# When ten attention tiles are begun inside the blocks of a feed-forward layer: five and five for six and four

## The chip, the cores and the metric

The kernel runs on one core of a Trainium2 chip, in one launch. The metric is the device time of the launch in microseconds (us). The kernel before was run three times: 846.51, 847.0 and 848.07 us, median 847.0 us. One more execution, the profiled one, took 846.59 us, and all rows below are from it.

## The reference

Chunked attention on 4 x 8 heads of 576 tokens (chunks of 64), then two feed-forward layers on the 2304 tokens that it gives, the first with softplus, the second with a rational function:

```python
scores = scale * np.matmul(q_c, k_c.transpose(0, 1, 2, 4, 3))      # per chunk of 64 tokens
attn = softmax(scores)                                             # max taken off, sum + 1e-9
x = matmul(attn, v_c)          # -> (2304 tokens, 512)
h = x @ w_in                   # 512 -> 2048
g = np.maximum(h, 0.0) + np.log1p(np.exp(-np.abs(h)))              # layer 1
x = g @ w_out                  # 2048 -> 512
h = x @ w_in2; g = P(h) / (Q(h) + 1e-6); out = g @ w_out2          # layer 2
```

Everything is fp32 in and out.

## The kernel before

**Numbers.** Each fp32 operand of a matmul is held as a sum of two fp32r parts, hi and lo, and each product takes three terms (hi hi, hi lo, lo hi). `split` (L397) makes the parts: ACT copies hi (L407), DVE or POOL subtracts it from the source for lo (L415).

**Tiles and blocks.** Attention works on 18 tiles of 128 tokens (tile 0 to 17). Layer 1 works on blocks of 512, 512, 512, 384 and 384 tokens, that is on tiles 0-3, 4-7, 8-11, 12-14 and 15-17. Blocks one to three run one after the other, each in 16 steps (fc 0 to 15); the products of step s = 16 * block + fc are called h_s (h_0 to h_47): 12 matmuls into one of two PSUM banks. ACT then makes softplus of them twice (L1142 into t2, L1147 into g, the hi part), DVE or POOL subtracts for the lo part (L1150), and 12 matmuls add g_s into the accumulators (L1656, "acc"). Blocks four and five are done together after them as a pair, by a scheme that needs sums and differences of their x (operands T, xT_4) and of the weights (s24, S1, S3), made beforehand by DVE and ACT (L1166 to L1430), and multiplied on PE by L1463 (p and u). Layer 2 follows, with its own blocks.

**Attention.** Tiles 0 to 7 are done at the start and in block one. The others are begun inside the blocks: `attention(tb)` is called in the loop over blocks and steps at the steps that BEGIN_AT lists, as many in each block as BEGUN says. A tile's work runs through DVE, PE and ACT: q and k are turned, PE makes scores (L718, L731), DVE takes the maximum and subtracts it (L756, L766), ACT takes exp (L776), sums and a divide follow (L800 to L811), PE transposes the weights e (L818), ACT copies them out (L840, "aT"), PE multiplies them with v (L847, L859, "values") into the PSUM tile "aps", and `split` writes the values as a part of xT. `attention` leaves this second half as `unfinished`; it is added by `finish_attention`, which the next tile's `attention` calls. So the finish of tile n is added where tile n+1 begins.

**The buffers of xT.** A block's xT is one of two buffers of the pool `xpool` (L341). A new one is taken by the copy of the block's first tile (`new_x`). Block four's xT (named xT_3, its first part is tile 12) takes the buffer of block two's (xT_1), which the products h_16 to h_31 read.

**What sets the order.** No engine's order is written out. The class `Program` records each task with its engine, an assumed cost, the keys that it reads and writes and the buffers that it takes, in the order in which the code adds them. A key that is written makes the task depend on the key's writer and on the readers known so far; readers and writers added later are tied to the new writer. A list scheduler with a random search over priorities then sets the order on all engines at once (L83 to L299). So a change of where a tile is begun changes the dependencies that the planner sees, and can change the order from the first instruction on.

Of the kernel before, what the change touches and what calls it, by code (L numbers as in the profile page):

```python
# [43 lines left out]
LAST_FINISH = 12  # L44
LEAD = 0.0
LEAD2 = 0.0
BEGUN = (0, 6, 4)
BEGIN_AT = ((), (0, 3, 6, 9, 11, 14), (0, 3, 6, 9))
CONVERT = ((), (1, 2, 4, 5, 7, 8, 10, 11, 12, 14, 15), (1, 2, 3, 4, 5))
BACK = (0, 0, 1, *(1,) * 13)  # L50
QK_BY_VECTOR = {*range(18)} - {*STAGED}
# [251 lines left out]
def tile_chunk_attention_two_ffn(  # L303
# [1537 lines left out]
    def tiles_of(j):  # L1841
        t0, n = BLOCKS[j]
        return range(t0 // TB, (t0 + n) // TB)
# [12 lines left out]
    for bi, j in enumerate(ORDER1):  # L1856
        later = [t for n in (*ORDER1[bi + 1 :], *PAIR) for t in tiles_of(n) if t not in STAGED + begun]
        coming = later[: BEGUN[bi]]
        begun += tuple(coming)
        for fc in range(FC):  # L1860
            s += 1
            if coming and fc in BEGIN_AT[bi]:
                tb = coming.pop(0)
# [174 lines left out]
```

## Time and profile before

| | us |
|---|---|
| median of three runs | 847.0 |
| profiled execution, its own time | 846.59 |
| its span (first to last instruction) | 844.8 |
| PE busy | 828.2 |
| DVE busy | 609.8 |
| ACT busy | 525.9 |
| POOL busy | 221.8 |

The profiled execution's own time has 1.8 us around its span. PE is the engine of the matrix products; the other three make its operands. The waits of PE that are listed one by one, and the chain of waits followed back from the last instruction, tell where PE did not go on; a stretch of time is read in the timelines of the engines beside it.

### The profile page before, as it was taken

How to read it: one execution, taken by the hardware profiler on the slowest of the kernel's cores; microseconds unless marked ns; L12 is line 12 of the kernel's file. 1: busy time of each engine (PE TensorE's matmuls, PEld its weight loads, DVE VectorE, ACT ScalarE, POOL GpSimd, SP SyncE). 2: the span in 40 equal slices, each digit the busy share in tenths (PEclk: the TensorE clock that was granted, in tenths of full speed). 3: DMA queues.
4: the chain of work that ended last, by engine and by line, in shares of the span. 5: the costliest groups of instructions: out<-in, count | busy, mean ns of one | idle time of the engine just before them, and what ended most of it. 6: DMA issues, size and time to landing. Idle time of an engine off the chain costs nothing.

```text
span 844.8 us, 13339 instructions
## 1 busy us (share of the span) xinstructions
PE 828.2 (98%) x4984; PEld 707.1 (84%) x4984; DVE 609.8 (72%) x1070; ACT 525.9 (62%) x934; POOL 221.8 (26%) x205
## 2 busy tenths in 40 slices
PE   7999999999799999999999999999999999999998
PEld 6778888888588889999998888888889888888886
DVE  5778774775565867565288996877888886778784
ACT  5898983332232345556448797776678775667674
POOL 0000002232222332111011488332235161312131
PEclk9899999999999999999999999999999999999999
DMA  9985535565455201000383242200031000001001
GB/s 228 248 222 178 191 80 159 138 141 142 113 133 125 82 1 51 1 1 1 133 257 110 75 125 76 76 1 1 0 107 44 1 26 1 1 0 51 1 0 50
DMA packets 112401, 71.13 MB, mean 84 GB/s; under 512 B 81872, under 2 KB 99792, under 8 KB 112336
## 3 DMA queue, kind: packets, MB, share of 16 engines
q1 hardware_dynamic: 112336, 70.28, 30.4%
q8 instruction: 39, 0.64, 0.3%
q14 instruction: 26, 0.21, 0.1%
HBM read 56.63 MB, written 13.63 MB: 83 GB/s over the span
## 4 chain that ended last, share of the span: by engine, by line
PE 90%; ACT 5%; DVE 3%; DMA 1%; issue 1%; POOL 0%; ACTq 0%; POOLq 0%; DVEq 0%
PE h L1075 36%; PE acc L1689 22%; PE acc L1656 22%; PE u L1463 3%; PE p L1463 3%; ACT L370 1%; PE aps L847 1%; DMA wr_1o<-in_moe_w_out_dram 1%; DVE t L1563 1%; PE aps L679 1%; PE aps L718 1%; PE aps L859 1%; PE warm L1992 1%; PE aps L818 0%; ACT t L1142 0%
## 5 line engine op out<-in xcount | busy, mean ns | idle before, releaser
L1075 PE MATMUL h<-xT,w_2i 128*128 128x512 f32 (+1 forms) x960 | 209.1, 368 | 0.0
L1689 PE MATMUL acc<-w_2o,g 128*128 128x512 f32 x864 | 207.9, 390 | 0.1
L1075 PEld LDWEIGHTS h<-xT,w_2i 128*128 128x128 f32 x960 | 169.0, 188 | 31.3 <-ACT u L1560 0.2
L1689 PEld LDWEIGHTS acc<-w_2o,g 128*128 128x128 f32 x864 | 161.3, 188 | 33.3 <-DVE w_2o L415 0.5
L1656 PE MATMUL acc<-g,w_1o 128*128 128x512 f32 (+1 forms) x768 | 176.6, 378 | 0.0
L1593 POOL TENSOR_TENSOR g<-t,g 128x512 fp32r<-128x512 f32 (+1 forms) x80 | 95.2, 1190 | 243.7 <-ACT g L1590 194.9
L1656 PEld LDWEIGHTS acc<-g,w_1o 128*128 128x128 f32 x768 | 140.5, 188 | 22.3
L1075 PE MATMUL h<-xT,w_1i 128*128 128x512 f32 x564 | 137.0, 394 | 5.3 <-ACT g L1147 5.3
L1075 PEld LDWEIGHTS h<-xT,w_1i 128*128 128x128 f32 x564 | 106.2, 190 | 28.1 <-ACT g L1147 5.8
L1582 ACT ACTIVATE u<-t,row 128x512 f32<-128x512 f32 (+1 forms) x80 | 51.8, 649 | 34.7 <-DVE t L1563 33.7
L1607 ACT ACTIVATE t<-h,row 128x512 f32<-128x512 f32 (+1 forms) x80 | 58.5, 731 | 21.7 <-PE h L1075 21.3
L1563 DVE SCALAR_TENSOR_TENSOR t<-t,row,u 128x512 f32<-128x512 f32 (+1 forms) x80 | 55.2, 691 | 20.6 <-ACT u L1586 20.2
L1618 DVE TENSOR_TENSOR t<-h,t 128x512 f32<-128x512 f32 (+1 forms) x80 | 50.8, 635 | 26.4 <-ACT u L1560 9.6
L1150 POOL TENSOR_TENSOR g<-t,g 128x512 fp32r<-128x512 f32 x32 | 41.6, 1300 | 103.0 <-ACT g L1147 103.0
L1563 DVE SCALAR_TENSOR_TENSOR t<-u,row,t 128x512 f32<-128x512 f32 (+1 forms) x80 | 55.4, 693 | 14.0 <-ACT t L1578 6.9
L1563 DVE SCALAR_TENSOR_TENSOR t<-t,row,h 128x512 f32<-128x512 f32 (+1 forms) x80 | 55.4, 692 | 12.6 <-ACT t L1578 7.5
L1142 ACT ACTIVATE t<-h 128x512 f32<-128x512 f32 x48 | 28.7, 598 | 52.1 <-PE h L1075 51.8
L1578 ACT ACTIVATE t<-h,row 128x512 f32<-128x512 f32 (+1 forms) x80 | 51.2, 641 | 15.3 <-PE h L1075 8.9
L1590 ACT ACTIVATE g<-t 128x512 fp32r<-128x512 f32 (+1 forms) x80 | 46.5, 581 | 16.9 <-DVE t L1563 13.9
L1563 DVE SCALAR_TENSOR_TENSOR u<-t,row,u 128x512 f32<-128x512 f32 (+1 forms) x80 | 55.6, 696 | 0.0
L1147 ACT ACTIVATE g<-h 128x512 fp32r<-128x512 f32 x48 | 28.6, 598 | 42.9 <-PE acc L1656 42.9
L1560 ACT ACTIVATE u<-h 128x512 f32<-128x512 f32 (+1 forms) x80 | 43.4, 544 | 17.7 <-DVE t L1563 6.6
(156 smaller groups left out, 1024.3 us busy)
## 6 DMA issues: line engine op xcount, KB each, us to landing
wr_1i<-in_moe_w_in_dram SPq DMA_DIRECT2D x16, 512.0 KB, 4.7
wr_1o<-in_moe_w_out_dram SPq DMA_DIRECT2D x16, 512.0 KB, 5.0
wr_2i<-in_moe_w_in_dram SPq DMA_DIRECT2D x16, 512.0 KB, 4.7
wr_2o<-in_moe_w_out_dram SPq DMA_DIRECT2D x16, 512.0 KB, 4.8
out_dram<-ev SPq DMA_DIRECT2D x16, 256.0 KB, 2.3
x<-ev SPq DMA_DIRECT2D x6, 512.0 KB, 3.4
x2r<-x SPq DMA_DIRECT2D x6, 512.0 KB, 4.0
qk<-in_q_dram SPq DMA_DIRECT2D x80, 32.0 KB, 3.2
```

The lines of the kernel that those rows point to most:

```text
L1075: pe.matmul(hs[s], w[:, a, c * P : (c + 1) * P], xt[:, b, c, :n_tok], start=n == 0, stop=n == 3 * KC - 1,)
L1463: pe.matmul(banks[n], lhs(a, i, c), right(b, j, c), start=start and m == 0, stop=m == 5, skip_group_check=not start,)
L1560: act.activation(u(), h(), AF.Square)
L1563: return lambda: vec.scalar_tensor_tensor(out=out(), in0=in0(), scalar=scalar, in1=in1(), op0=op0, op1=op1)
L1578: act.activation(new("t1"), h(), AF.Abs, scale=b_t[:, 0:1])
L1582: act.activation(u(), d(), AF.Ln, bias=epsq_t)
L1590: act.activation(gs[s][:, 0, :n_tok], p(), AF.Copy)
L1593: pool.tensor_tensor(out=gs[s][:, 1, :n_tok], in0=p(), in1=gs[s][:, 0, :n_tok].bitcast(F32), op=ALU.subtract,)
L1607: lambda: act.activation(new("t2"), h(), AF.Identity, scale=na_t[:, 3:4], bias=na_t[:, 2:3]),
L1618: lambda: vec.tensor_tensor(out=p(), in0=h(), in1=p(), op=ALU.mult), [hkey, kp], [kp],
L1656: pe.matmul(accs[1, j, half][c % 2][:, :n_tok], wts[1, "o", fc][:, a, c * P : (c + 1) * P], gs[s][:, b, :n_tok], start=first and n == 0, s ...
L1689: pe.matmul(accs[2, j, half][c % 2], gs[s][:, b, c * P : (c + 1) * P], wts[2, "o", fc][:, a, :], start=first and n == 0, stop=last and n == 2,
```

## The change

Tiles 8 to 17 are the ten that are begun inside blocks two and three. Before, six began in block two, at steps 0, 3, 6, 9, 11 and 14, and four in block three, at steps 0, 3, 6 and 9. Now five begin in each: tiles 8 to 12 at steps 0, 3, 6, 9 and 12 of block two, tiles 13 to 17 at steps 0, 2, 4, 6 and 8 of block three. Tile 12 is begun a step later, tile 13 two steps later and in the next block; tile 14 is begun at step 2 instead of 0, tile 15 at 4 instead of 3, tile 16 stays at 6, and tile 17 begins at 8 instead of 9.

```diff
-BEGUN = (0, 6, 4)
-BEGIN_AT = ((), (0, 3, 6, 9, 11, 14), (0, 3, 6, 9))
+BEGUN = (0, 5, 5)
+BEGIN_AT = ((), (0, 3, 6, 9, 12), (0, 2, 4, 6, 8))
```

No instruction of the computation is added or removed; the table loads of ACT (L370) are 23 instead of 25, and the small matmuls that keep PE going at the start (L1992) stand in another place. The planner's order differs on every engine. Three places follow.

**Around tile 12's copy, ACT.** The copy of tile 12's values into block four's xT (L407, xT_3), before: t2 and g are the softplus outputs of the products of the same number, cm_2i and cm_2o conversions of layer 2's weights, e_13 the exp of tile 13.

```order
L470 ACTIVATE cm_2o_12_2399<-wr_2o_12_2335 128x512
L407 ACTIVATE xT_3_2408<-aps_513 128x4x128
L776 ACTIVATE e_13_2442<-e_13_2442,row_97 128x512
L1142 ACTIVATE t2_30_2464<-h_1_30_2428 128x512
L1147 ACTIVATE g_30_2468<-h_1_30_2428 128x512
L1147 ACTIVATE g_31_2490<-h_1_31_2449 128x512
L1142 ACTIVATE t2_31_2492<-h_1_31_2449 128x512
```

And now:

```order
L1142 ACTIVATE t2_30_2368<-h_1_30_2332 128x512
L1142 ACTIVATE t2_31_2385<-h_1_31_2354 128x512
L470 ACTIVATE cm_2i_13_2401<-wr_2i_13_2371 128x512
L1147 ACTIVATE g_30_2413<-h_1_30_2332 128x512
L1147 ACTIVATE g_31_2446<-h_1_31_2354 128x512
L1142 ACTIVATE t2_32_2462<-h_1_32_2433 128x512
L1147 ACTIVATE g_32_2488<-h_1_32_2433 128x512
L470 ACTIVATE cm_2o_13_2491<-wr_2o_13_2464 128x512
L1142 ACTIVATE t2_33_2501<-h_1_33_2475 128x512
L1728 ACTIVATE ev_1_1_0_2510<-acc_1_1_0_1580 128x512
L1728 ACTIVATE ev_1_1_1_2547<-acc_1_1_1_0_1610 128x512
L1147 ACTIVATE g_33_2552<-h_1_33_2475 128x512
L407 ACTIVATE xT_3_2571<-aps_497 128x4x128
```

The copy xT_3 stood ahead of the softplus of h_30 and h_31; now it stands behind the last of g_33. The conversion cm_2o_12 stands in front of t2_30 in the one as in the other.

**The same place, PE.** Here aT_12 and v_12 give the values of tile 12, qkT_13 the scores of tile 13. Before:

```order
L847 MATMUL aps_513<-aT_12_2323,v_12_2294 64x64 x16
L718 MATMUL aps_513<-qkT_13_2291 64x64 x16
L1656 MATMUL acc_1_1_0_1620<-g_29_2346,w_1o_13_1352 128x512 x6
L1656 MATMUL acc_1_1_1_0_1604<-g_29_2346,w_1o_13_1352 128x512 x3
L1656 MATMUL acc_1_1_1_1_1605<-g_29_2346,w_1o_13_1352 128x512 x3
L1075 MATMUL h_1_30_2428<-xT_1_770,w_1i_14_1350 128x512 x12
L1075 MATMUL h_1_31_2449<-xT_1_770,w_1i_15_1417 128x512 x12
L1075 MATMUL h_1_32_2477<-xT_2_1745,w_1i_0_121 128x512 x12
L1656 MATMUL acc_1_1_1_0_1604<-g_30_2468,w_1o_14_1424 128x512 x3
```

And now:

```order
L1075 MATMUL h_1_30_2332<-xT_1_802,w_1i_14_1366 128x512 x12
L1075 MATMUL h_1_31_2354<-xT_1_802,w_1i_15_1439 128x512 x12
L1656 MATMUL acc_1_1_0_1580<-g_28_2265,w_1o_12_1324 128x512 x6
L1656 MATMUL acc_1_1_1_0_1610<-g_28_2265,w_1o_12_1324 128x512 x3
L1656 MATMUL acc_1_1_1_1_1611<-g_28_2265,w_1o_12_1324 128x512 x3
L1656 MATMUL acc_1_1_0_1580<-g_29_2346,w_1o_13_1373 128x512 x6
L1656 MATMUL acc_1_1_1_0_1610<-g_29_2346,w_1o_13_1373 128x512 x3
L1656 MATMUL acc_1_1_1_1_1611<-g_29_2346,w_1o_13_1373 128x512 x3
L1075 MATMUL h_1_32_2433<-xT_2_1796,w_1i_0_121 128x512 x12
```

The values of tile 12 stood ahead of h_30 and are no longer among these rows (they come after the sums of g_31); between h_31 and h_32 there was nothing, and now there are six groups of sums (24 matmuls).

**Block one, around the transposes of tile 6 (L679).** On PE the transposes of e_5 (L818) come first, then sums, then those of tile 6, which take the same PSUM tile. Before:

```order
L818 MATMUL aps_513<-ident_96,e_5_772 128x128 x4
L1656 MATMUL acc_1_0_1_0_589<-g_4_780,w_1o_4_784 128x512 x3
L1656 MATMUL acc_1_0_1_1_590<-g_4_780,w_1o_4_784 128x512 x3
L679 MATMUL aps_513<-ident_96,qk_6_119 128x128 x8
L1075 MATMUL h_1_6_865<-xT_0_331,w_1i_6_127 128x512 x12
```

And now:

```order
L818 MATMUL aps_497<-ident_96,e_5_797 128x128 x4
L1656 MATMUL acc_1_0_1_0_558<-g_4_799,w_1o_4_785 128x512 x3
L1656 MATMUL acc_1_0_1_1_559<-g_4_799,w_1o_4_785 128x512 x3
L1656 MATMUL acc_1_0_0_578<-g_4_799,w_1o_4_785 128x512 x6
L679 MATMUL aps_497<-ident_96,qk_6_119 128x128 x8
L1656 MATMUL acc_1_0_1_0_558<-g_5_852,w_1o_5_847 128x512 x3
```

Three groups of sums (12 matmuls) stand between the two transposes instead of two (6 matmuls). On ACT, from the exp of tile 5 to the copy aT_5 that empties that PSUM tile, before:

```order
L776 ACTIVATE e_5_772<-e_5_772,row_97 128x512
L370 ACT_TABLE_LOAD
L468 ACTIVATE cm_1i_6_802<-wr_1i_6_683 128x512
L468 ACTIVATE cm_1o_5_805<-wr_1o_5_713 128x512
L468 ACTIVATE cm_1i_7_813<-wr_1i_7_759 128x512
L468 ACTIVATE cm_1o_6_815<-wr_1o_6_782 128x512
L370 ACT_TABLE_LOAD
L1147 ACTIVATE g_5_827<-h_1_5_789 128x512
L407 ACTIVATE w_1i_6_127<-cm_1i_6_802 128x512
L840 ACTIVATE aT_5_846<-aps_513 128x512
```

And now:

```order
L776 ACTIVATE e_5_797<-e_5_797,row_97 128x512
L370 ACT_TABLE_LOAD
L468 ACTIVATE cm_1i_7_825<-wr_1i_7_773 128x512
L468 ACTIVATE cm_1o_6_828<-wr_1o_6_787 128x512
L407 ACTIVATE w_1o_5_847<-cm_1o_5_730 128x512
L370 ACT_TABLE_LOAD
L1147 ACTIVATE g_5_852<-h_1_5_806 128x512
L1142 ACTIVATE t2_5_861<-h_1_5_806 128x512
L840 ACTIVATE aT_5_870<-aps_497 128x512
```

Four weight conversions (L468) stood there and now two, and one hi copy of a weight (L407) and one softplus (L1142) stand on other sides of the copy than before.

**The end of block three, PE.** From the values of tile 17 (aT_17), the last tile, on (p and u are products of the pair). Before:

```order
L847 MATMUL aps_513<-aT_17_3305,v_17_3184 64x64 x16
L1075 MATMUL h_1_47_3356<-xT_2_1745,w_1i_15_1417 128x512 x12
L1656 MATMUL acc_1_2_1_0_2615<-g_44_3294,w_1o_12_1332 128x512 x3
L1656 MATMUL acc_1_2_1_1_2616<-g_44_3294,w_1o_12_1332 128x512 x3
L1656 MATMUL acc_1_2_0_2604<-g_45_3321,w_1o_13_1352 128x512 x6
L1656 MATMUL acc_1_2_1_0_2615<-g_45_3321,w_1o_13_1352 128x512 x3
L1656 MATMUL acc_1_2_1_1_2616<-g_45_3321,w_1o_13_1352 128x512 x3
L1463 MATMUL p_0_0_3417<-xT_3_2408,w_1i_0_121 128x384 x6
L1656 MATMUL acc_1_2_0_2604<-g_46_3400,w_1o_14_1424 128x512 x6
L1656 MATMUL acc_1_2_1_0_2615<-g_46_3400,w_1o_14_1424 128x512 x3
L1656 MATMUL acc_1_2_1_1_2616<-g_46_3400,w_1o_14_1424 128x512 x3
L1656 MATMUL acc_1_2_0_2604<-g_47_3424,w_1o_15_1476 128x512 x6
```

And now:

```order
L847 MATMUL aps_497<-aT_17_3337,v_17_3226 64x64 x16
L1656 MATMUL acc_1_2_1_0_2583<-g_45_3323,w_1o_13_1373 128x512 x3
L1656 MATMUL acc_1_2_1_1_2584<-g_45_3323,w_1o_13_1373 128x512 x3
L1656 MATMUL acc_1_2_0_2600<-g_46_3379,w_1o_14_1446 128x512 x6
L1656 MATMUL acc_1_2_1_0_2583<-g_46_3379,w_1o_14_1446 128x512 x3
L1656 MATMUL acc_1_2_1_1_2584<-g_46_3379,w_1o_14_1446 128x512 x3
L1656 MATMUL acc_1_2_0_2600<-g_47_3418,w_1o_15_1457 128x512 x6
L1656 MATMUL acc_1_2_1_0_2583<-g_47_3418,w_1o_15_1457 128x512 x3
L1656 MATMUL acc_1_2_1_1_2584<-g_47_3418,w_1o_15_1457 128x512 x3
L1463 MATMUL p_0_0_3456<-xT_3_2571,w_1i_0_121 128x384 x6
L1463 MATMUL u0_3473<-xT_3_2571,w_1i_2_123 128x384 x6
L1463 MATMUL p_0_1_3485<-xT_3_2571,w_1i_0_121 128x384 x6
```

The values of tile 17 stand behind h_47 instead of ahead of it and behind sums of g_45; after the rows shown, before, come six more sums of g_47, then u0, six products of T2, six of xT_3 and six of T3 ahead of the first product that reads xT_4, and now u1 alone stands ahead of that product.

At the start, two subtractions of DVE (L766) for the fourth starting tile stand behind the divide of the second (L811), where they stood ahead of it, and all 24 pieces of h_0 (L1100) stand behind the last starting tile's values (L859), where 8 stood ahead of them.

## Rows read from the trace of the kernel before

**Rows 1.** Head of the page: span; busy us, share and instructions of PE.
```profile
span 844.8 us, 13339 instructions
...
PE 828.2 (98%) x4984; PEld 707.1 (84%) x4984; DVE 609.8 (72%) x1070; ACT 525.9 (62%) x934; POOL 221.8 (26%) x205
```

**Rows 2.** Section 4 of the page: the chain of waits, shares by engine.
```profile
PE 90%; ACT 5%; DVE 3%; DMA 1%; issue 1%; POOL 0%; ACTq 0%; POOLq 0%; DVEq 0%
```

**Rows 3.** Waits of PE: who waits, releaser, us in total, times, longest.
```profile
PE h L1075 <- ACT g L1147: 5.3, 1, 5.3
PE aps L818 <- DVE room L811: 2.6, 1, 2.6
...
PE aps L679 <- ACT aT L840: 0.8, 1, 0.8
```

**Rows 4.** The chain in order of time: start us, us, what.
```profile
210.00 5.45 PE h L1075 x24
...
219.66 0.58 ACT t L1142
...
220.78 4.50 PE h L1075 x12
```

**Rows 5.** ACT's timeline: start us, us, instruction, [idle <- releaser].
```profile
207.28 0.68 ACT L470 ACTIVATE cm_2o<-wr_2o 128x512 f32<-128x512 f32 x1 [2.21 <-DMA w2i<-cm_2i]
215.48 0.60 ACT L407 ACTIVATE xT<-aps 128x512 fp32r<-128x512 f32 x1 [7.52 <-PE h L1075]
219.03 0.72 ACT L776 ACTIVATE e<-e,row 128x512 f32<-128x512 f32 x1 [2.95 <-DVE e L766]
```

**Rows 6.** Windows: PE, PEld, DVE, ACT, POOL busy us, PEclk, DMA share, GB/s.
```profile
221.00:223.00 2.00, 2.00 (x5) 1.61 (x6) 1.31 (x2) 1.36 (x3) 1.66 (x2) 0.50 0.78 127
...
225.00:229.00 4.00, 4.00 (x20) 3.28 (x19) 3.80 (x8) 1.20 (x2) 0.21 (x1) 1.00 0.73 172
```

**Rows 7.** PE's timeline, block one, around the transposes of tile 6.
```profile
60.26 1.64 PE L1656 MATMUL acc<-g,w_1o 128*128 128x512 f32 x6
62.74 1.09 PE L679 MATMUL aps<-ident,qk 128*128 128x128 f32 x8 [0.85 <-ACT aT L840]
```

**Rows 8.** ACT's timeline, the same stretch.
```profile
57.42 0.68 ACT L468 ACTIVATE cm_1i<-wr_1i 128x512 f32<-128x512 f32 x1
...
59.79 1.28 ACT L370 ACT_TABLE_LOAD   x1
...
62.10 0.59 ACT L840 ACTIVATE aT<-aps 128x512 f32<-128x512 f32 x1
```

**Rows 9.** DVE's timeline at the start.
```profile
16.88 0.41 DVE L766 TENSOR_TENSOR room<-aps,mx 128x256 f32<-128x256 f32 x1
```

**Rows 10.** ACT's timeline at the start.
```profile
24.36 0.60 ACT L840 ACTIVATE room<-aps 128x512 f32<-128x512 f32 x1 [0.42 <-PE aps L818]
```

**Rows 11.** PE's timeline at the start.
```profile
23.98 2.06 PE L1100 MATMUL h<-xT,w_1i 128*128 128x256 f32 x8
25.96 0.69 PE L859 MATMUL aps<-room,v 64*64 64x64 f32 x32
26.59 2.04 PE L1100 MATMUL h<-xT,w_1i 128*128 128x256 f32 x12
28.99 0.74 PE L1100 MATMUL h<-xT,w_1i 128*128 128x256 f32 x4 [0.36 <-DVE xT L1006]
```

**Rows 12.** PE's timeline before the pair of blocks.
```profile
308.03 0.69 PE L847 MATMUL aps<-aT,v 64*64 64x64 f32 x32
```

**Rows 13.** DVE's timeline before the pair of blocks.
```profile
313.38 2.39 DVE L1368 TENSOR_TENSOR r<-w_1i 128x512 f32<-128x512 f32 x2
...
318.07 0.68 DVE L1269 TENSOR_TENSOR xT<-xb,xT 128x512 fp32r<-128x512 f32 x1
...
322.87 0.69 DVE L1368 TENSOR_TENSOR r<-w_1i 128x512 f32<-128x512 f32 x1
```

**Rows 14.** POOL's timeline, the same stretch.
```profile
313.87 1.36 POOL L1150 TENSOR_TENSOR g<-t,g 128x512 fp32r<-128x512 f32 x1 [7.85 <-ACT g L1147]
```

## The prediction

> **What bounds the kernel now.** I read the head of the page first: PE is busy for 828.2 of a span of 844.8 us [rows 1]. The chain of waits agrees, 90% PE, 5% ACT, 3% DVE [rows 2]. With 16.6 us of the span not PE's, a change of order alone can only win in the places where PE stands still, or lose by making new ones. So the next view is the list of PE's waits. One of them is far larger than the rest after the start: 5.3 us ahead of a product h, with ACT's softplus g named as the releaser. Of the others, 2.6 us are the start's, for DVE's divide, and 0.8 us is a wait of the transposes L679 for ACT's copy aT [rows 3].
>
> The chain in order of time shows how the 5.3 us come about. PE works on h_30 and h_31 until 210.00 + 5.45 = 215.45. Then the chain leaves PE: the softplus of h_30 starts only at 219.66, and PE goes on at 220.78 with h_32, which needs one of the two banks of h_30 and h_31 [rows 4]. ACT had nothing to do meanwhile: its copy into xT stood at the head of its queue and waited 7.52 us for PE's h. Behind it stood tile 13's exp, which waited another 2.95 us for DVE's subtraction of the maximum, and only then the softplus of h_30 [rows 5]. So this is a ring. The copy takes the buffer that h_30 and h_31 read, and cannot start before h_31 ends; the softplus that would free the banks is queued behind the copy, although h_30 was ready 2.7 us earlier.
>
> The stop costs more than its idle time. The windows show a granted clock of 0.50 from 221 to 223, the lower of the two levels (1.2 of 2.4 GHz), after PE had idled, and 1.00 again from 225 [rows 6]. h_32 takes 4.50 us, while h_30 and h_31 take 5.45 together, 2.72 each [rows 4].
>
> **The change part by part.**
>
> *The ring.* Before, tile 13 was begun at step 14 of block two, so tile 12's finish, with the copy into xT_3, was recorded before h_30 and h_31 were. The planner then knew of no reading of the old buffer by these two, and put ACT's copy ahead of their softplus. The chip's semaphores hold it all the same. Now tile 13 begins at step 0 of block three, behind all sixteen products of block two, and the order shows the copy behind g_33's softplus. t2_30 and g_30 stand with nothing of tile 12 or 13 ahead of them. What goes is the idle time, 220.78 - 215.45 = 5.33 us, and the slow clock, 4.50 - 2.72 = 1.78 us: **-7.1 us**.
>
> What is late next there? h_32 needs the bank of h_30. In the new order h_31 (2.72 us) and 24 matmuls of sums (24 x 0.227 = 5.45 us, by 5.45 / 24 from [rows 4]) stand between the end of h_30 and h_32: 8.2 us of work. ACT needs for t2_30, t2_31, a conversion and g_30 four times about 0.6 us, 2.4 us. The cover is some 5.8 us, so I take the whole sum. The copy itself, later now, holds only the values of tile 12, which nobody needs before the pair of blocks. Bounds: -7.1 if the cover holds, 0 if something else holds ACT there for the same time.
>
> *Block one.* PE's six matmuls of sums from 60.26 would end at 61.62 (6 x 0.227), and the transposes start at 62.74 [rows 7]: 1.12 us lost. They wait for the PSUM tile that ACT's copy aT empties at 62.10 to 62.69. Ahead of the copy ACT does four conversions (the first at 57.42), a table load of 1.28 us, and softplus [rows 8]. Now two of the four conversions are gone from there, a second softplus has come in, and PE has 12 sums to do, 2.72 us instead of 1.36. PE gains 1.36 of cover and ACT about one instruction of 0.56 us, together 1.9 us against 1.12 lost: **-1.1 us**, with 0 as the other bound, if the later h_5 or DVE's part of tile 5 is what ends last.
>
> *The start.* In DVE's queue two subtractions of 0.41 us [rows 9] go behind the divide of the second starting tile, for which PE waited 2.6 us [rows 3]; it comes about 0.7 us earlier. In exchange eight pieces of h_0, which took 2.06 us [rows 11] while ACT's copy was still to come, go behind the last starting tile's values. That copy ended at 24.36 + 0.60 = 24.96 [rows 10], the pieces at 25.96, so the values can start 1.0 us earlier, and 24 pieces instead of 16 follow. At 2.04 / 12 = 0.17 us a piece [rows 11] h_0 would end at 24.96 + 0.63 + 24 x 0.17 = 29.67, which is where it ends now (28.99 + 4 x 0.17). Of the 0.7 us I believe half, since some conversions moved ahead of the last tile's divide: **-0.4 us**. Bounds: -1.1 us (all of the 0.7, and the 0.36 of waiting in [rows 11]) and +1.7 us (24 pieces at the 2.06 / 8 = 0.26 of the first eight cost 2.1 more, less the 0.4).
>
> *The end of block three.* From the values of tile 17 at 308.03 [rows 12] DVE and ACT make the operands of the pair, the last of them xT's lo part at 318.07 + 0.68 [rows 13]: 10.7 us. Before, PE had 54 matmuls of 0.227 us and 30 of 128x384 (0.227 x 384 / 512 = 0.17 us each) in that time, 17.4 us by the order, before the first product that reads xT_4. Now the values stand behind h_47: 30 sums (6.8 us) and 24 small products (4.1 us) remain, 10.9 us. The margin falls from 6.7 us to 0.2. Against that the operands S and s24 are asked for in another order. I take **+0.4 us**: at most a small wait, since the chain of 10.7 holds work for other operands that the new order can put behind. Bounds: 0 and about +3.
>
> Row and rule here: two subtractions of DVE took 2.39 us while POOL made a softplus's lo part beside them, from 313.87 on [rows 14]; one alone takes 0.69 [rows 13]. The Trainium skill, "GPSIMD Engine Reference", section "1. Specifications", says that GpSimd shares its SBUF interfaces with VectorE, with contention for DVE instructions that have two SBUF inputs, as these have; the trace agrees. It speaks against the change: tile 17's operands are subtractions of that sort, and they now run nearer to the softplus of h_46 and h_47.
>
> *All the rest* (blocks two and three besides, the pair, layer 2) is reordered without a visible cost: PE had hardly a wait there, and the new order has no two products of h that stand closer than others did before. I take 0, with +-1 us for small waits that come or go.
>
> Sum: 846.59 - 7.1 - 1.1 - 0.4 + 0.4 = 838.4 us for an execution like the profiled one. The median is 847.0, 0.4 more, so the forecast is **838.8 us**. All terms at their good ends give 846.6 - 7.1 - 1.1 - 1.1 - 1 + 0.4 = 836.7.
>
> **The rivals.**
>
> *The pair of blocks waits.* The margin of 0.2 us does not hold: DVE's chain behind tile 17's values is stretched by POOL's lo parts, by 1.1 us for each that falls on two subtractions (2.39 less twice about 0.65). With two or three of them PE waits 2 to 3 us ahead of the first product with xT_4; and as the stop at 215 shows, PE's clock may fall after it and cost up to 1.8 more. Time: 841 to 843.5 us, say 842. For it: the order has values later, and five tiles in block three. Against it: products that don't need xT_4 are at hand, and the searching planner puts them in front.
>
> *The change does not do what it says.* The copy is free, but ACT is held elsewhere by another instruction at the head of its queue, such as the exp of a tile that waits for DVE (2.95 us before, [rows 5]), and PE stands for as long as before: 845.3 to 848.7, about 847. Against it: the cover of 5.8 us.
>
> *Slower: the conversion in front of the softplus.* cm_2o_12 stands right ahead of t2_30 in the new order. It waits for a DMA, and ACT waits in order; one such wait was 2.2 us, just before the copy [rows 5]. PE waits for what its lateness exceeds the cover of 5.8 us by, and 1.8 us go to the clock. Slower than before by 1.7 us it is from 5.8 + 8.2 (the sum of the four terms) + 1.7 - 1.8 = 13.9 us on; at 15 us the time is 838.8 + 9.2 + 1.8 = 849.8, about 850. Against it: no wait of that kind was longer than 2.2 us.
>
> **How the numbers follow.** Three runs of before span 1.6 us, and 0.2% (1.7 us) is about what can be told from no change. The forecast has 0.72, with its own range 836.5 to 840.5; the pair's wait 0.15; no change 0.07; slower 0.06. The first two are faster by over 0.2%: 0.87. The range leaves out the last two and a little at the low end: 836 to 843.5 us.
>
> **What would show it.** In the list of PE's waits the row h <- g of 5.3 us is gone, the windows around the passage from block two to three have a clock of 1.00 throughout, and h_32 takes 2.7 us. ACT's copy of tile 12 starts without a long wait. The row L679 <- aT of 0.8 us is gone. At the end of block three a wait of p (L1463) for DVE's xT, s or S of up to 0.5 us agrees with my term; 2 us or more is the first rival. PE's busy time falls by about 1.8 us and the span by about 8. The forecast is wrong if a wait of over 3 us stands anywhere after the start, or if the copy of xT_3 is still ahead of a softplus for which PE waits.

## The result and the profile after

The changed kernel takes 840.08 us (median of four runs, 839.73 to 840.27), the kernel before 847.48 us in the same comparison (846.51 to 848.07): a ratio of 0.9913, 95% interval 0.9896 to 0.993. It is 7.4 us faster; the forecast was 838.8 us, 1.3 us too low, within its range. In a later comparison the same two took 841.22 and 847.24 us, a ratio of 0.993 (0.9918 to 0.9943).

The head of the page after, section 4 (the chain of waits by engine) and PE's waits (who waits, releaser, us in total, times, longest) answer to [rows 1 to 3]:

```profile
span 838.0 us, 13379 instructions
...
PE 827.4 (99%) x5004; PEld 707.6 (84%) x5004; DVE 611.0 (73%) x1070; ACT 523.2 (62%) x932; POOL 224.0 (27%) x205
```

```profile
PE 96%; SPq 1%; ACT 1%; DMA 1%; DVE 0%; issue 0%
```

```profile
PE aps L818 <- DVE room L811: 2.0, 1, 2.0
PE warm L1992 <- DVE xT L415: 1.4, 1, 1.4
...
PE aps L859 <- ACT room L840: 0.9, 2, 0.7
PE p L1463 <- ACT u L1484: 0.6, 1, 0.6
```

The chain is on PE for 96% instead of 90%, and ACT's share has gone from 5% to 1%. The wait of h for g (5.3 us) and that of L679 for aT (0.8 us) are gone. Two are new: the small matmuls "warm" wait 1.4 us for DVE at the start, and the pair of blocks 0.6 us. PE's instructions are 5004 instead of 4984, and all 20 are such small matmuls: the section on the change says that they stand in another place, but there are 48 of them instead of 28. The program counts them from the gaps that the planner leaves on PE before the first h.

PE's timeline at the passage to block three (start us, us, instruction) answers to [rows 4]:

```profile
203.39 5.60 PE L1075 MATMUL h<-xT,w_1i 128*128 128x512 f32 x24
208.83 5.60 PE L1656 MATMUL acc<-g,w_1o 128*128 128x512 f32 x24
214.27 2.88 PE L1075 MATMUL h<-xT,w_1i 128*128 128x512 f32 x12
216.99 2.88 PE L1656 MATMUL acc<-g,w_1o 128*128 128x512 f32 x12
```

h_30 and h_31 are followed by 24 matmuls of sums and by h_32 without a gap. On ACT, answering to [rows 5]:

```profile
204.33 0.66 ACT L470 ACTIVATE cm_2o<-wr_2o 128x512 f32<-128x512 f32 x1
206.31 0.60 ACT L1142 ACTIVATE t<-h 128x512 f32<-128x512 f32 x1 [1.32 <-PE h L1075]
...
226.47 0.60 ACT L407 ACTIVATE xT<-aps 128x512 fp32r<-128x512 f32 x1 [0.47 <-PE aps L718]
```

The softplus of h_30 starts when its products end, and the copy of tile 12 comes 23 us after the start of h_30 instead of 5.6, with a wait of 0.47 us instead of 7.52. The windows (PE, PEld, DVE, ACT, POOL busy us, PEclk, DMA share, GB/s) show the full clock there, where [rows 6] had 0.50:

```profile
209.00:215.00 6.00, 6.00 (x28) 4.95 (x28) 5.80 (x11) 2.21 (x4) 1.62 (x1) 1.00 0.40 73
215.00:221.00 6.00, 6.00 (x28) 4.99 (x27) 1.06 (x2) 1.75 (x4) 1.66 (x2) 1.00 0.52 155
```

**Where the time went.** The profiled executions have spans of 844.8 and 838.0 us, 6.8 apart. I compare them at points where PE has done the same work of the computation.

| stretch | before | after | difference |
|---|---|---|---|
| end of h_0 | 29.57 | 30.97 | +1.4 |
| start of tile 6's transposes (after: 65.87 less 2.72 for h_6, which stands ahead of them now) | 62.74 | 63.15 | +0.4, so block one -1.0 |
| start of h_30 to end of h_32 (after: less the 24 sums, 5.44) | 225.11 - 209.84 = 15.27 | 216.99 - 203.39 - 5.44 = 8.16 | -7.1 |
| all the rest | | | -0.1 |

Block one answers to [rows 7]: the transposes (L679) follow the sums without a wait.

```profile
62.66 0.60 PE L818 MATMUL aps<-ident,e 128*128 128x128 f32 x4
63.01 3.02 PE L1656 MATMUL acc<-g,w_1o 128*128 128x512 f32 x12
65.87 1.03 PE L679 MATMUL aps<-ident,qk 128*128 128x128 f32 x8
```

On ACT ([rows 8]) the copy that frees their PSUM tile ends at 63.89, two microseconds before they start:

```profile
60.94 1.28 ACT L370 ACT_TABLE_LOAD   x1
62.24 0.60 ACT L1147 ACTIVATE g<-h 128x512 fp32r<-128x512 f32 x1
62.73 0.59 ACT L1142 ACTIVATE t<-h 128x512 f32<-128x512 f32 x1
63.29 0.60 ACT L840 ACTIVATE aT<-aps 128x512 f32<-128x512 f32 x1
```

The start, PE's timeline, answers to [rows 11]:

```profile
17.30 0.65 PE L818 MATMUL aps<-ident,room 128*128 128x128 f32 x4 [1.96 <-DVE room L811]
...
21.21 2.07 PE L1992 MATMUL warm<-ident 128*128 128x128 f32 x8 [1.44 <-DVE xT L415]
23.08 1.06 PE L818 MATMUL aps<-ident,room 128*128 128x128 f32 x4
...
27.90 3.23 PE L1100 MATMUL h<-xT,w_1i 128*128 128x256 f32 x24
30.97 1.04 PE L679 MATMUL aps<-ident,qk 128*128 128x128 f32 x8
```

The second starting tile's transposes come at 17.30 instead of 17.95. But behind its values stand eight small matmuls, which write the PSUM tile of these values and so wait for DVE's subtraction that reads it; the third tile's transposes follow at 23.08, 5.78 us after the second's, where they came 2.41 us after them before (17.95 and 20.36).

### The profile page after: what moved, and what is told of

The parts are those of the page before. It is cut to its first block, busy times and chain, and to the rows that moved or that the text cites. A ratio compares the mean times of both kernels' runs of the same rounds, so it can differ in the third digit from the quotient of the medians.

```text
span 838.0 us, 13379 instructions
## 1 busy us (share of the span) xinstructions
PE 827.4 (99%) x5004; PEld 707.6 (84%) x5004; DVE 611.0 (73%) x1070; ACT 523.2 (62%) x932; POOL 224.0 (27%) x205
## 4 chain that ended last, share of the span: by engine, by line
PE 96%; SPq 1%; ACT 1%; DMA 1%; DVE 0%; issue 0%
PE h L1075 39%; PE acc L1656 24%; PE acc L1689 23%; PE p L1463 3%; PE u L1463 3%; SPq L622 1%; PE aps L847 1%; DMA wr_1i<-in_moe_w_in_dram 1%; PE aps L718 1%; PE aps L859 0%; PE aps L679 0%; PE warm L1992 0%; PE h L1100 0%; PE aps L818 0%; SPq L643 0%; PE aps L731 0%
## 5 line engine op out<-in xcount | busy, mean ns | idle before, releaser
L1075 PE MATMUL h<-xT,w_1i 128*128 128x512 f32 x564 | 135.2, 391 | 0.0
L1150 POOL TENSOR_TENSOR g<-t,g 128x512 fp32r<-128x512 f32 x32 | 43.6, 1362 | 126.1 <-ACT g L1147 126.1
L1142 ACT ACTIVATE t<-h 128x512 f32<-128x512 f32 x48 | 28.6, 596 | 59.4 <-PE h L1075 59.2
```

Source lines behind the costliest of these rows:

```text
L1075: pe.matmul(hs[s], w[:, a, c * P : (c + 1) * P], xt[:, b, c, :n_tok], start=n == 0, stop=n == 3 * KC - 1,)
L1150: (vec if by_vector else pool).tensor_tensor(out=gs[s][:, 1, :n_tok], in0=t["t2"], in1=gs[s][:, 0, :n_tok].bitcast(F32), op=ALU.subtract,)
```

## The experiments

My theory is the ring: tile 12's finish is recorded ahead of the products h_30 and h_31, so ACT's copy stands ahead of the softplus that PE needs, while it waits for PE. The rivals are that the even spread of the tiles pays, that tile 13's exp behind the copy was the real stop, and that the new search of the planner was lucky.

**e1: the ring put back into the changed kernel.**

```diff
-BEGUN = (0, 5, 5)
-BEGIN_AT = ((), (0, 3, 6, 9, 12), (0, 2, 4, 6, 8))
+BEGUN = (0, 6, 4)
+BEGIN_AT = ((), (0, 3, 6, 9, 12, 14), (2, 4, 6, 8))
```

> The changed kernel with tile 13 begun at step 14 of block two again (six and four tiles; all other places as in the changed kernel). Theory (the ring: tile 12's finish is recorded ahead of h_30 and h_31, so ACT's copy xT_3 stands ahead of their softplus): the wait of h for g of about 5.3 us at the passage to block three is back, with a slow h_32 behind it, and the time is 7.1 us above the changed kernel's 840.1, about 847 us. Rival (the gain comes from spreading the tiles five and five, or from the new search as a whole): no wait above 2 us there, 839 to 842 us.

It took 846.18 us, 0.9982 of before (0.9973 to 0.9991), a little under the expected 847. The stop is back, as PE's timeline and then ACT's show:

```profile
209.54 5.60 PE L1075 MATMUL h<-xT,w_1i 128*128 128x512 f32 x24
219.66 4.61 PE L1075 MATMUL h<-xT,w_1i 128*128 128x512 f32 x12 [4.52 <-ACT g L1147]
```

```profile
215.18 0.60 ACT L407 ACTIVATE xT<-aps 128x512 fp32r<-128x512 f32 x1 [6.19 <-PE h L1075]
...
218.54 0.58 ACT L1142 ACTIVATE t<-h 128x512 f32<-128x512 f32 x1
```

The copy again stands ahead of the softplus of h_30, and h_32 again takes 4.61 us. 4.52 + 4.61 - 2.72 = 6.4 us are lost, near the 6.1 by which its median stands above the changed kernel's.

**e2: before, with two instructions moved.** `done[12]` is DVE's subtraction of tile 12's values, the task ahead of it ACT's copy. Both have to go: in DVE's queue the subtraction stood ahead of tile 13's maximum, which tile 13's exp needs, and waited 8.37 us for the copy.

```diff
-        for i, t in prog.schedule():
+        order = prog.schedule()
+        late = [o for o in order if o[0] in (done[12] - 1, done[12])]
+        order = [o for o in order if o not in late]
+        at = [i for i, t in order].index(g31) + 1      # g31: ACT's task for g_31
+        order[at:at] = late
+        for i, t in order:
```

> The kernel before with its own order on every engine, but for two instructions: the copy of tile 12's values into xT_3 (ACT) and its subtraction (DVE) are issued behind g_31 instead of ahead of t2_30. Theory (ring): the wait of 5.3 us and the slow h_32 go, nothing else moves, 847.5 - 7.1 = 840.4 us; ACT's copy waits for less than 1 us. Rival (the stop has another cause, such as tile 13's exp that waits for DVE, which stays ahead of t2_30): PE still stands for 2 to 5 us, 843 to 847 us.

839.68 us, 0.9907 of before (0.9892 to 0.9922), where the ring said 840.4. This shows the cause: begin steps, search and the rest of the order are those of before, and the gain is there. PE's timeline and ACT's:

```profile
210.46 8.32 PE L1075 MATMUL h<-xT,w_1i 128*128 128x512 f32 x36
218.62 4.24 PE L1656 MATMUL acc<-g,w_1o 128*128 128x512 f32 x18
```

```profile
211.47 0.73 ACT L776 ACTIVATE e<-e,row 128x512 f32<-128x512 f32 x1 [1.15 <-DVE e L766]
...
213.88 0.59 ACT L1147 ACTIVATE g<-h 128x512 fp32r<-128x512 f32 x1
216.16 0.60 ACT L1147 ACTIVATE g<-h 128x512 fp32r<-128x512 f32 x1 [1.69 <-PE h L1075]
216.66 0.59 ACT L407 ACTIVATE xT<-aps 128x512 fp32r<-128x512 f32 x1
```

h_30, h_31 and h_32 are one run of 36 matmuls, 8.16 us from start to start of what follows, against 15.27 before: -7.1 us to the tenth. Tile 13's exp stands ahead of the softplus as before and does no harm, since it no longer comes behind the copy. One other wait moved: that of L679 for aT in block one was 1.67 us here, with the order of before, where it had been 0.85.

**e3: tile 13 alone moved** in the kernel before (tile 14 makes room by one step).

```diff
-BEGIN_AT = ((), (0, 3, 6, 9, 11, 14), (0, 3, 6, 9))
+BEGIN_AT = ((), (0, 3, 6, 9, 11), (0, 1, 3, 6, 9))
```

> The kernel before with tile 13 alone moved: begun at step 0 of block three, tile 14 at step 1 to make room; tiles 12 and 15 to 17 stay where they were. Theory (ring): 847.5 - 7.1 = 840.4, with 1.5 us to either side for what the search finds elsewhere: 839 to 842 us, no wait of PE above 1 us after the start. Rival (the regular spacing of the tiles in block three matters as well): ACT and DVE are late with tiles 13 and 14 begun one step apart, waits of 2 us or more in block three, 843 us or more.

839.43 us, 0.9912 (0.9898 to 0.9925), and no wait above 0.8 us behind the start. In these times the places of tiles 12 and 15 to 17 win nothing; the section on e4, e7 and e8 looks behind the start.

**e9: tile 13 one step later** in the kernel before.

```diff
-BEGIN_AT = ((), (0, 3, 6, 9, 11, 14), (0, 3, 6, 9))
+BEGIN_AT = ((), (0, 3, 6, 9, 11, 15), (0, 3, 6, 9))
```

> The kernel before with tile 13 begun at step 15 of block two instead of 14, nothing else: h_30 is now recorded ahead of tile 12's finish, h_31 still behind it. Theory (ring): the softplus of h_30 stands ahead of the copy, that of h_31 behind it, so half of the ring is left. h_32 starts at once in the bank of h_30; h_33 waits for h_31's bank, which comes free 5.3 us after the end of h_31 as before, less the 2.7 us of h_32: a wait of 2.6 us, and 0 to 1.8 us of low clock. 847.3 - 7.1 + 2.6 = 842.8 to 844.6 us. Rival (what matters is that tile 13 leaves block two): 846 to 848 us, the wait of 5.3 us as before.

844.26 us, 0.997 (0.996 to 0.9979), within the expected 842.8 to 844.6. PE's timeline, then ACT's:

```profile
213.79 5.60 PE L1075 MATMUL h<-xT,w_1i 128*128 128x512 f32 x24
221.19 3.06 PE L1075 MATMUL h<-xT,w_1i 128*128 128x512 f32 x12 [1.80 <-ACT t L1142]
```

```profile
216.71 0.60 ACT L407 ACTIVATE xT<-aps 128x512 fp32r<-128x512 f32 x1 [8.82 <-PE h L1075]
219.44 0.72 ACT L776 ACTIVATE e<-e,row 128x512 f32<-128x512 f32 x1 [2.14 <-DVE e L766]
```

h_31 and h_32 run through, and h_33 waits 1.80 us for the bank of h_31, not 2.6: DVE gave the exp its input 2.14 us after the copy instead of 2.95. From the start of h_31 to the end of h_33 224.08 - 213.79 - 8.16 = 2.1 us are lost, and two further waits, 1.0 us for an aT of tile 13 and 0.4 us, follow. So half a ring costs about half of the 7.1 us: the tile's block is not what decides, but which products are recorded ahead of its begin. That the time is within the range is partly luck: three waits in layer 2 (0.7, 0.4 and 0.2 us), which e3 has too, add to it.

**e5 and e6: a new search.** Each kernel with other seeds (`range(100, 100 + self.SEEDS)`).

> The kernel before with other seeds of the planner's random search (100 to 119 instead of 0 to 19), nothing else. It shows what a new search alone does. Theory (ring: it follows from what is recorded when, not from luck of the search): the copy stands ahead of the softplus of h_30 in this order too, PE waits for 4.5 to 5.5 us at the passage to block three, 845.5 to 848.5 us. Rival (the gain of the change is a luckier search): this kernel falls anywhere between 839 and 847 us, below 844 us as likely as not, without the wait.

> The changed kernel with other seeds of the planner's random search (100 to 119 instead of 0 to 19), nothing else. Theory (ring): no wait above 2 us at the passage to block three; the start and the small waits differ, 838.5 to 841.5 us. Rival (luck of the search): the gain is lost in part, 843 us or more.

Before with new seeds took 848.05 us (ratio 1.0016, 1.0006 to 1.0025), and one row of PE's waits says why:

```profile
PE h L1075 <- ACT g L1147: 5.0, 1, 5.0
```

The changed one took 841.4 us (0.9931, 0.9917 to 0.9945), without it. New seeds moved the kernel before by 1.1 us (848.05 against 846.96); the changed one, at 0.9931, stands where its later comparison had it (0.993) and 1.5 us above the first (0.9913). With two searches for each, the ring was there or not as the begin steps say.

**e4, e7, e8: the start of the changed kernel.** e4 leaves out the 20 added small matmuls, which belong to no output:

```diff
-                x["warm"] = ps_att.tile([P, 2, 512], F32, tag="att", name="warm_2")[:, 0]
+                x["warm"] = None
```

e7 puts the first two of h_0's six tasks (eight pieces) ahead of the last starting tile's values in the order found, and e8 does both.

```diff
+        first = [o for o in order if o[0] in pieces][:2]       # pieces: the six tasks of h_0
+        at = order.index(first[0])
+        while prog.tasks[order[at - 1][0]][0] != PE:
+            at -= 1
+        order = [o for o in order if o not in first]
+        order[at - 1 : at - 1] = first
```

> The changed kernel without the 20 small matmuls (L1992) behind the second starting tile's values; these write the PSUM tile of that tile's values and wait 1.44 us for DVE's subtraction that reads it. Theory (they hold the third tile's transposes up, at 23.08 us instead of about 20.5 when DVE's divide is done): h_0 ends 1.2 us earlier than the 30.97 us of the changed kernel, between 0 and 2 us, 838.9 us. Rival (they keep PE's clock up, and without them the transposes and the 24 pieces of h_0 run at the lower level): the start is as long or up to 1.5 us longer, 840 to 841.6 us.

> The changed kernel's order with the first eight pieces of h_0 put ahead of the last starting tile's values again, as before the change (the last four of the 20 small matmuls go with that, since they end with the first piece). Theory (the pieces fill PE's time while ACT copies, so moving them behind the values made the start longer): h_0 ends at about 30.2 us instead of 30.97, 839.4 us. Rival (the values of the last tile are what ends last, as the prediction had it): the pieces hold the values up, h_0 ends at 30.9 to 32 us, 840 to 841 us.

> Both edits of the start together: the changed kernel without the 20 small matmuls behind the second starting tile and with the first eight pieces of h_0 ahead of the last starting tile's values. If both costs are real and add up, h_0 ends at 29.6 to 29.9 us instead of 30.97, 838.9 us, the best version so far of this order. Rival (PE's clock at the lower level takes it back): h_0 ends at 30.2 us or later, no faster than the one without the small matmuls alone, 839.9 to 840.5 us.

They took 840.25 (838.95 to 842.19), 841.07 and 839.74 us: ratios 0.9918, 0.993 and 0.9912, with intervals that overlap the changed kernel's. All three are above what was expected (838.9, 839.4 and 838.9), e4 inside its rival's range and e7 at the edge of its own. The times settle little, so I measure from the second tile's transposes to the end of h_0, which leaves out when the first data came:

| kernel | transposes | h_0 ends | between |
|---|---|---|---|
| before | 17.95 | 29.57 | 11.6 |
| after | 17.30 | 30.97 | 13.7 |
| after again (e10) | 17.93 | 32.58 | 14.7 |
| e4, without the small matmuls | 17.10 | 30.15 | 13.1 |
| e8, and eight pieces ahead | 18.08 | 30.79 | 12.7 |
| e3 and e11, tile 13 alone moved | 17.02, 17.04 | 28.74, 28.57 | 11.7, 11.5 |

Behind h_0 the changed kernel, e10, e4, e7 and e8 all take 806.9 to 807.1 us to the end of the span, so these five differ in the start alone. The kernel before takes 815.2 there, e3 and e11 808.6 (837.3 - 28.74 and 837.2 - 28.57). So behind the start the changed kernel is 1.6 us ahead of the one with tile 13 alone moved; 1.3 us of that are the three waits in layer 2 that e9 has too. Whether the tiles' places or the search took them away is not shown.

e4 is 0.6 us shorter than the changed kernel; its rows show that the clock takes some back, 24 pieces in 4.14 us instead of 3.23:

```profile
20.45 1.11 PE L818 MATMUL aps<-ident,room 128*128 128x128 f32 x4 [0.88 <-DVE room L811]
...
26.18 4.14 PE L1100 MATMUL h<-xT,w_1i 128*128 128x256 f32 x24
```

From 26 to 28 us the granted clock was 0.50 in e4 and 1.00 in the changed kernel.

e7 failed as an experiment: the count of small matmuls follows the planned times, and moving the pieces brought eight more in front of them (12 instead of 4), so h_0 ended at 32.63. e8 is free of that and gains 0.3 on e4. But the two executions of the changed kernel are 1.0 us apart in the table, so neither gain is shown.

**e10 and e11: the best version beside the changed kernel on one chip.**

> The changed kernel again, for comparison with the next on one chip: 840.1 us, ratio to before 0.9913.

> The kernel before with tile 13 alone moved (step 0 of block three, tile 14 at step 1), beside the changed kernel on one chip. Theory (the start of the changed kernel, with 20 small matmuls more and all pieces of h_0 behind the last values, costs 1 to 2 us that this one does not pay, and the rest is equal): 0.5 to 1.5 us below the changed kernel, 838.6 to 839.6. Rival (the places of the other tiles win something too): the same time or longer.

841.22 us (839.94 to 841.88) against 839.31 (838.98 to 840.07): the one with tile 13 alone moved is 1.9 us faster in this comparison, more than the 1.5 expected. But its ratio to before is 0.9913 (0.9899 to 0.9926) against 0.993 (0.9918 to 0.9943), and these overlap; in the first comparisons the two kernels stood level (0.9912 and 0.9913). So that it beats the changed kernel is not shown. The start makes up more than all of the 1.9 us, 14.7 against 11.5 in the table; behind it the changed kernel is 1.6 us ahead.

## Why the prediction was right, and where it was off

**The ring: right, and in size too.** The forecast was -7.1 us, the traces and e2 give -7.1. That the copy with its subtraction, not tile 13's exp, was the stop is shown by e2; that it follows from the order of recording, by e1, e5 and e9. The cover of 5.8 us held, and the slow rival did not come: the conversion cm_2o_12 ran at 204.33 without a wait, 2.0 us ahead of the softplus that needs ACT.

**Block one: right, the size partly by luck.** -1.0 us measured, -1.1 forecast, and the copy aT now ends 2.0 us ahead of the transposes that need it, as the cover said. But the wait that went was 0.85 us in one execution of the old order and 1.67 in another (e2).

**The start: the term that was mis-sized.** -0.4 us forecast, +1.4 measured; this is more than the whole error of 1.3 us. One half was right: DVE's divide frees the second tile 0.65 us earlier (17.95 to 17.30, forecast 0.7). What failed is the step "so the values can start 1.0 us earlier", which took the end of the last copy, 24.96, from the old trace. In the new one that copy ends at 27.23 and the values start at 27.28, 2.3 us later than forecast; the 24 pieces behind them then take 3.07 us (30.97 - 27.90) instead of the 4.08 of the sum. From the second tile's transposes to the end of h_0 the changed kernel needs 2.1 us more than the one before. The delay arises at the third tile. DVE's rows of the changed kernel:

```profile
17.23 0.42 DVE L766 TENSOR_TENSOR room<-aps,mx 128x256 f32<-128x256 f32 x1
...
18.03 0.42 DVE L766 TENSOR_TENSOR room<-aps,mx 128x256 f32<-128x256 f32 x1
18.37 0.68 DVE L483 SCALAR_TENSOR_TENSOR cm_1i<-wr_1i,cm_1i 128x512 uint32<-128x512 uint32 x1
...
19.75 0.68 DVE L811 TENSOR_TENSOR room<-room,sm 128x512 f32<-128x512 f32 x1
```

The two subtractions that let the second tile's divide pass, and a conversion, now stand ahead of the third's, which ends at 20.43 instead of 19.74. Without the small matmuls the third tile's transposes still come 3.35 (e4) and 3.64 us (e8) after the second's instead of 2.41. This part, some 1 us, was read, not tried. The small matmuls, which I had not counted, hold the same transposes up by 2.4 us more (5.78 against 3.35), and the clock gives 1.8 of that back by the end of h_0 (from these transposes on 7.89 us against 9.70 in e4). That leaves 0.6 us for them, and e8 0.3 for the pieces; both are below what two executions of the changed kernel differ by, so how the rest is shared stays open.

**The pair of blocks: right in size by luck, the cause was another.** I had +0.4 us for late operands of tile 17, 10.7 us of chain against 10.9 us of products. The rows after, DVE's and PE's ([rows 12, 13]):

```profile
311.20 0.68 DVE L1269 TENSOR_TENSOR xT<-xb,xT 128x512 fp32r<-128x512 f32 x1
...
318.35 0.69 DVE L1407 TENSOR_TENSOR s<-r,s 128x512 fp32r<-128x512 f32 x1
318.95 2.11 DVE L1368 TENSOR_TENSOR r<-w_1i 128x512 f32<-128x512 f32 x2
```

```profile
306.64 0.69 PE L847 MATMUL aps<-aT,v 64*64 64x64 f32 x32
...
318.39 1.21 PE L1463 MATMUL p<-xT,S 128*128 128x384 f32 x6
319.44 1.21 PE L1463 MATMUL p<-T,s 128*128 128x384 f32 x6
321.23 1.31 PE L1463 MATMUL p<-T,S 128*128 128x384 f32 x6 [0.58 <-ACT u L1484]
```

The chain took 311.88 - 306.64 = 5.2 us, not 10.7: in the old order DVE had weight differences between its links ([rows 13]). The product that reads xT_4 starts 6.5 us after it is ready, so the first rival did not come. What stood close is the weights' operand s, ready at 319.04, 0.4 us ahead of the product that reads it. The wait of 0.58 us is for ACT to read a product out of its bank (u, L1484), and stands behind that product. Two subtractions of DVE again took 2.11 us while POOL worked beside them for 1.16 us from 319.35 on; it cost PE nothing here. The Trainium skill ("GPSIMD Engine Reference", section "1. Specifications") says that DVE instructions with two SBUF inputs contend with GpSimd; the trace agrees, since one such subtraction alone took 0.68 us at 314.34.

**The range and the other marks.** The list of waits, the clock and h_32's 2.7 us came as said. PE's busy time fell by 0.8 instead of 1.8 us: the small matmuls took 9.5 us instead of 5.6, and the pieces of h_0, at a higher clock, 3.2 instead of 4.8.

## What to carry to other kernels

When an engine stands idle at the head of its queue while PE waits for what is queued behind, look for a ring: a copy into a reused buffer, ahead of the work that lets the buffer's last readers finish. A planner that learns of dependencies in the order of recording sees only the readers recorded so far; a buffer's new owner must be recorded behind its last reader; one step too early already cost about half of the stop here. After a search has laid the order anew, read the start and every stage again: terms of 1 to 2 us of either sign came with it here, and instructions that are counted from the plan's gaps did so too.

## What the runs showed of the hardware

Stops of PE of 4.52 us (e1), 4.99 (e5) and 5.33 (before) each left the following 12 matmuls at 4.5 to 4.9 us instead of 2.72. After a stop of 1.80 us (e9) h_33 took 2.9, and the window behind it had the full clock:

```profile
218.00:222.00 4.00, 2.20 (x10) 1.48 (x9) 3.00 (x7) 2.56 (x6) 0.53 (x1) 1.00 0.93 289
222.00:224.00 2.00, 2.00 (x10) 1.64 (x9) 1.44 (x3) 0.66 (x2) 2.00 (x3) 1.00 0.00 0
```

So a stop of 5.3 us cost 7.1, and one of 1.8 us cost 2.1, each measured over three products h against 8.16 us.

The start varies between executions of one kernel: the changed one needed 13.7 and 14.7 us for the same instructions, with a wait of the small matmuls of 1.44 and 1.81 us; from 23 to 26 us the granted clock was 0.71 in the one and 0.50 in the other, from 26 to 28 us 1.00 and 0.57.
